# Expert layers of a recurrence-and-two-MoE kernel: second router in common operations for up to four tiles, expert rows in units of 32, sort moved between the two products

## The chip, the cores and the metric

One core of one Trainium2 chip. The metric is the device time of one execution in microseconds (us), the median of several executions.

## The reference, cut to what matters

A recurrence over 768 steps (4 batches, 8 heads of 40) gives 3072 rows of 320 values. Two mixture-of-experts layers follow, each with 8 experts of 320 x 1024 and 1024 x 320 weights, each row going to the expert of its largest logit. The second layer has a capacity of 768 rows per expert.

```python
def _moe_ref(x, w_gate, w_output_gate, w1, w2):
    logits = x @ w_gate
    e_idx = np.argmax(logits, axis=1)
    ...
    for e in range(E):
        mask = e_idx == e
        h = np.maximum(x[mask] @ w1[e], 0.0)
        ye = h @ w2[e]
        out[mask] = gate_w[mask, None] * eom[mask, e, None] * ye

def _moe2_ref(x, w_gate, w1, w2, capacity):
    logits = x @ w_gate
    expert_idx = np.argmax(logits, axis=1)
    probs = softmax(logits)
    gate_w = probs[np.arange(N), expert_idx]
    ...
    # each expert takes its rows in order, up to capacity; out = gate_w * relu(x @ w1[e]) @ w2[e]
```

## The kernel before

The recurrence comes first, in 24 chunks of 128 rows. Each finished chunk is routed for layer 1 (logits, choice of expert, rank within the expert, gate) and scattered by an indirect DMA to its expert's region of a DRAM table, `xs1`. Layer 1 works through this table expert by expert and scatters its rows, routed for layer 2, into `xs2`. Layer 2 does the same and scatters its rows to the output.

**Slots and blocks.** Experts are sorted by their number of rows into 8 slots, and a slot has a fixed number of rows: `NU1` and `NU2` (L721 to L722) count them in units of 64. A slot's rows are cut into blocks of up to four tiles of 128 rows (`Layer`, L764 to L779); the last tile of a block may have 64. The first slot of a layer is cut in two, so that its first block (`HEAD1`, `HEAD2`) can begin before all rows are there. Layer 1 has the blocks 0 to 8 (block 2 is the second slot, block 8 the last), layer 2 the blocks 9 to 18. Rows beyond an expert's count are zero. Were an expert to have more rows than its slot, a branch behind the two layers would compute the rest, tile by tile, with weights loaded anew.

**One block** (`stream`, L1079). The first product (`first`, L1035) has eight steps f = 0 to 7. Each is 8 matmuls (L1050) of a 128 x 128 weight piece with all the block's rows as columns (the high and low parts of an fp32 value are multiplied separately), into one of three PSUM buffers `hp`. ScalarE then writes `hh` (L1052) and VectorE `hl` (L1053). The second product (`second`, L1058) takes the tiles j one by one, with 24 matmuls of 320 columns each (L1072, again eight steps f), into one of two PSUM buffers `yp`. Then the epilogue of the tile runs: ScalarE scales the result into `x2` (L1369), VectorE copies 64 columns to pad it (L1370). In layer 2 ScalarE writes `y` (L1383) and GpSimd scatters it.

**What is put between the steps.** `between(phase, f)` (L1153) runs side work behind the matmuls of step f. The letters are `e` (one step of every waiting router), `l` (load the rows of the next block), `x` (transpose and split a tile of the next block, L1025 to L1029), `w` (convert a third of a weight matrix to high and low parts, L993/L994 and L1006/L1007, then fetch the next third to the freed buffer). `PLAN` (L748) gives the places for blocks 0, 1, 2, 9 and 10. For the others `FT`, `FL`, `FW` give the steps in the first product, and `ST`, `SX`, `SW` those in each tile of the second. `hooks` (L1468) runs the sort of the experts (`order`, L929), the choice of the two leading experts (`leads`, L961) and the table counts (`left`, L1428) before or in the middle of given blocks. From block 0 on every engine, and the queue on which SyncE (SP) issues the DMAs, executes its instructions in the order in which the code issues them.

**The router of layer 2** (`route2` L910, `route` L797) runs for one tile in three steps. First three transposes of `x2` on TensorE (L803) and a copy of the result by ScalarE (L805). Second the logits (three fp32 matmuls, L809, six in the profile) and five VectorE operations to the choice `oh` (L812 to L822). Third two matmuls for the ranks (L832, L833), then ten VectorE operations and an exponential, and the scatter (L919).

## Time and profile before

| | |
|---|---|
| median of 3 executions | 954.26 us (951.37 to 959.03) |
| profiled execution | 947.28 us, of which the span from first to last instruction is 945.5 us |
| mean granted TensorE clock | 0.931 |
| busy: TensorE matmul, weight load | 808.0 us (85%), 716.8 us (76%) |
| busy: VectorE, ScalarE, GpSimd | 665.9 us (70%), 502.5 us (53%), 301.5 us (32%) |
| matmuls of the first product (L1050), second (L1072) | 1216, 1296 |

Times in the profile are us from the start of the span. The recurrence fills some 456 us and overlaps block 0. Block 2 begins at 508.56, block 9 (layer 2) at 727.53, block 10 at 752.61, and the last matmul is at 932. A matmul row shows when it starts and how long it runs, and successive matmuls overlap, so the cost of a matmul in a stream is the distance of the starts.

### The profile page before, as it was taken

The page shows a single profiled execution, that of the slowest core. Times are in us where ns is not written, and L with a number is a line of the kernel's source. Part 1 is how long each engine was busy: PE and PEld are TensorE (multiplying, and loading weights), DVE is VectorE, ACT ScalarE, POOL GpSimd, SP SyncE. Part 2 cuts the span into 40 slices and gives each one's busy share as a digit, 9 for nine tenths or more (in the row PEclk, how much of TensorE's full clock was granted, in tenths as well). Part 3 has the DMA queues.
Part 4 walks back from the last instruction along what each step waited for, and adds up shares of the span by engine and source line. Part 5 has one row for each costly group of instructions (what it writes and reads, how often), then busy time and mean ns, then how long its engine had stood idle before and what let it go on. Part 6 is the DMA issues. An engine that isn't in the chain of part 4 may idle for free. (4 is left out here: it accounts for less than half of the span.)

```text
span 945.5 us, 31326 instructions
## 1 busy us (share of the span) xinstructions
PE 808.0 (85%) x12638; PEld 716.8 (76%) x12638; DVE 665.9 (70%) x1902; ACT 502.5 (53%) x1241; POOL 301.5 (32%) x465
## 2 busy tenths in 40 slices
PE   8357678878879778969999999999899999999994
PEld 4236567756767667757798888999898989999994
DVE  6999966996996976752676767767777844556561
ACT  6225467756857747759443543545355444445551
POOL 8835545645555644223120111111101111101120
PEclk9757789989989879989999999999999999999998
DMA  6759777687665633355353525535445434625640
GB/s 169 195 120 252 212 181 197 174 225 216 162 156 129 154 76 98 89 132 159 115 142 109 151 62 148 141 93 155 132 140 159 140 112 143 193 66 175 180 142 22
DMA packets 132853, 137.50 MB, mean 145 GB/s; under 512 B 68388, under 2 KB 114183, under 8 KB 132700
## 3 DMA queue, kind: packets, MB, share of 16 engines
q1 hardware_dynamic: 128140, 121.99, 48.4%
q0 software_dynamic: 4560, 13.43, 3.9%
q8 instruction: 102, 1.67, 0.8%
q14 instruction: 51, 0.42, 0.1%
HBM read 91.25 MB, written 28.68 MB: 127 GB/s over the span
## 5 line engine op out<-in xcount | busy, mean ns | idle before, releaser
L1072 PE MATMUL yp<-w2h,hh 128*128 128x320 f32 (+1 forms) x432 | 139.4, 327 | 0.6 <-ACT hh L1052 0.6
L919 POOL DMA_INDIRECT xs<-x,di x52 | 55.4, 1065 | 260.2 <-ACT xh L1027 94.9
L1053 DVE SCALAR_TENSOR_TENSOR hl<-hp,hh 128x384 fp32r<-128x384 f32 (+5 forms) x152 | 77.6, 517 | 80.0 <-ACT hh L1052 78.5
L1072 PE MATMUL yp<-w2l,hh 128*128 128x320 f32 (+1 forms) x432 | 132.7, 311 | 0.0
L1050 PE MATMUL hp<-xh,w1h 128*128 128x384 f32 (+5 forms) x456 | 126.3, 335 | 2.7 <-ACT xh L1027 2.1
L1050 PE MATMUL hp<-xh,w1l 128*128 128x384 f32 (+5 forms) x456 | 124.3, 327 | 0.0
L1072 PE MATMUL yp<-w2h,hl 128*128 128x320 f32 (+1 forms) x432 | 112.2, 309 | 0.0
L1052 ACT ACTIVATE hh<-hp 128x384 fp32r<-128x384 f32 (+5 forms) x152 | 68.2, 459 | 81.0 <-PE hp L1050 78.0
L252 DVE TENSOR_TENSOR X<-X,tmp 128x112 f32<-128x112 f32 (+19 forms) x186 | 81.2, 437 | 5.6
L250 DVE TENSOR_TENSOR tmp<-N,X 128x112 f32<-128x112 f32 (+19 forms) x186 | 81.0, 437 | 5.0
L1050 PEld LDWEIGHTS hp<-xh,w1h 128*128 128x128 f32 x456 | 79.8, 191 | 5.5 <-ACT xh L1027 2.6
L1050 PEld LDWEIGHTS hp<-xh,w1l 128*128 128x128 f32 x456 | 81.9, 189 | 2.1
L451 POOL TENSOR_TENSOR YL<-uvs,mlow 64x512 f32<-64x512 f32 x44 | 58.3, 1326 | 76.8 <-ACT uvs L448 70.9
L1072 PEld LDWEIGHTS yp<-w2h,hh 128*128 128x128 f32 (+1 forms) x432 | 79.9, 185 | 2.0 <-ACT hh L1052 0.8
L1072 PEld LDWEIGHTS yp<-w2l,hh 128*128 128x128 f32 (+1 forms) x432 | 79.6, 184 | 0.6
L919 POOL DMA_INDIRECT out_dram<-y,ti x26 | 26.5, 1018 | 165.3 <-DVE ti L1346 32.5
L1050 PE MATMUL hp<-xl,w1h 128*128 128x384 f32 (+5 forms) x304 | 74.8, 327 | 0.4 <-DVE xl L1028 0.2
L1072 PEld LDWEIGHTS yp<-w2h,hl 128*128 128x128 f32 (+1 forms) x432 | 73.8, 183 | 0.4
L102 PE MATMUL ps<-wb 128*128 128x512 bf16 x217 | 72.7, 421 | 1.4 <-POOL wb L95 1.1
L994 DVE TENSOR_TENSOR w1l<-ws,w1h 128x1024 fp32r<-128x1024 f32 x48 | 58.5, 1221 | 20.7 <-ACT w1h L993 14.3
L414 PE MATMUL ps<-consts,T 104*104 104x104 f32 x368 | 46.3, 272 | 19.2 <-ACT KBS L416 17.5
L414 PEld LDWEIGHTS ps<-consts,T 104*104 104x104 f32 x368 | 38.7, 140 | 24.6 <-ACT KBS L416 21.6
(267 smaller groups left out, 1801.3 us busy)
## 6 DMA issues: line engine op xcount, KB each, us to landing
xt<-xs SPq DMA_DIRECT2D x49, 193.0 KB
kb<-in_kb_dram SPq DMA_DIRECT2D x24, 360.0 KB
ws<-in_w_dram SPq DMA_DIRECT2D x16, 512.0 KB
ws<-in_v_dram SPq DMA_DIRECT2D x16, 512.0 KB
xs<-z SPq DMA_DIRECT2D x8, 965.0 KB
KBS<-KBI SPq DMA_DIRECT2D x48, 160.0 KB
ws<-in_w_dram SPq DMA_DIRECT2D x16, 480.0 KB
ws<-in_v_dram SPq DMA_DIRECT2D x16, 480.0 KB
```

The lines of the kernel that those rows point to most:

```text
L102: pin(matmul(wps, wb, wb.unsqueeze(1).to_broadcast([128, 4, 128]), **whole))
L250: nc.vector.tensor_tensor(out=tmp, in0=N[:, j:j + 1, i].to_broadcast([128, m, n]), in1=X[:, k, j:j + 1].to_broadcast([128, m, n]), op=ALU. ...
L252: nc.vector.tensor_tensor(out=X[:, k, i], in0=X[:, k, i], in1=tmp, op=ALU.add)
L414: pin(transpose(sp[0:104, h, 0:104], t1[0:104, i, h0 + h], ident[0:104, 0:104]))
L451: (nc.vector if last else nc.gpsimd).tensor_tensor(out=yl[q, 2 * cl:2 * cl + 2], in0=s[q].rearrange("p (i h t) -> p i h t", i=2, h=H), in1 ...
L919: self.nc.gpsimd.indirect_dma_start(out=dst, out_offset=bass.IndirectOffsetOnAxis(ap=di[:, 0:1], axis=0), in_=src, in_offset=None, bounds_ ...
L994: return lambda: nc.vector.tensor_tensor(out=t["w1l"][:, k], in0=s, in1=t["w1h"][:, k].bitcast(F32), op=ALU.subtract)
L1050: nc.tensor.matmul(hp[:, 0:n], a, b, start=(i == 0), stop=(i == len(ops) - 1))
L1052: nc.scalar.activation(hh[:, f, 0:n], hp[:, 0:n], AF.Relu)
L1053: nc.vector.scalar_tensor_tensor(out=hl[:, f, 0:n], in0=hp[:, 0:n], scalar=0.0, in1=hh[:, f, 0:n].bitcast(F32), op0=ALU.max, op1=ALU.subtract)
L1072: nc.tensor.matmul(yp[0:m, 0:DM], a[:, g, c], w[b][:, g], start=(f == i == 0), stop=(f == 7 and i == 2))
```

## The change

Four things change together.

- Slots are counted in units of 32 rows. Layer 1's slots go from 448, 448, 448, 448, 384, 384, 384, 384 rows to 448, 448, 416, 416, 384, 384, 384, 352. Layer 2's go from 512, 512, 640, 384, 384, 320, 256, 256 to 512, 480, 640, 384, 384, 320, 256, 224. The heads keep 320 and 384 rows. The number of tiles stays 28 and 26, since a short tile is still a tile.
- The second router works on all tiles of a block together. Tile by tile it transposes, now with the logits of the tile before in the same step. When all logits are there, one chain of VectorE operations chooses for up to four tiles, and one pair of rank matmuls, one exponential and one chain of VectorE operations end it. Then come a reciprocal and a scatter for each tile.
- `leads` and `left` run in the middle of their blocks (7 and 3), between the two products, where they ran before them.
- Router steps stand at other places (`FT`, `ST`, `PLAN`), and the load of block 10 moves from step 2 to step 6 of block 9.

```diff
-UNIT = 64
-NU1 = (7, 7, 7, 7, 6, 6, 6, 6)
-NU2 = (8, 8, 10, 6, 6, 5, 4, 4)
-HEAD1, HEAD2 = 5, 6
+UNIT = 32
+PER = 128 // UNIT
+NU1 = (14, 14, 13, 13, 12, 12, 12, 11)
+NU2 = (16, 15, 20, 12, 12, 10, 8, 7)
+HEAD1, HEAD2 = 10, 12
...
-FT, FL, FW = (0, 1, 3), 3, ((), (2, 4, 6))
-ST, SX, SW = (2, 5), (3,), (0, 4)
+FT, FL, FW = (0, 2, 6), 3, ((), (2, 4, 6))
+ST, SX, SW = (2,), (3,), (0, 4)
...
-    9: ({0: 'e', 1: 'e', 2: 'l', 3: 'w', 4: 'w', 6: 'ew', 7: 'w'}, {0: 'w', 1: 'w', 5: 'e', 6: 'x', ...
+    9: ({0: 'e', 2: 'e', 3: 'w', 4: 'w', 6: 'elw', 7: 'w'}, {0: 'w', 1: 'w', 9: 'w', 17: 'w', 20: 'x', 23: 'w'}),
...
+    def route2(self, P, pools, X, tk, n, wg, seen, xs):
+        nc, v = self.nc, self.nc.vector
+        ps, sb = pools
+        lp = ps.tile([128, 512], F32, tag="rt", name="lp")
+        lq, lr = (lp[:, q:q + 8 * n] for q in (384, 416))
+        def logits(j, xT):
+            for k in range(3):
+                self.pin(nc.tensor.matmul(lq[:, 8 * j:8 * j + 8], xT[:, 128 * k:128 * k + 128], wg[:, k], ...
+        turned, xT = 0, None
+        while turned < n:
+            if turned < len(X):
+                if turned:
+                    logits(turned - 1, xT)
+                for k in range(3):
+                    self.pin(nc.tensor.transpose(lp[:, 128 * k:128 * k + 128], X[turned][:, 128 * k:128 * k + 128], self.ident))
+                xT = sb.tile([128, 384], F32, tag="rxT", name="xT")
+                self.pin(nc.scalar.copy(xT, lp[:, 0:384]))
+                turned += 1
+            yield
+        logits(n - 1, xT)
...
+        v.reduce_max(m.unsqueeze(2), lg, axis=AX.X)
+        v.tensor_tensor(out=ex, in0=lg, in1=wide(m), op=ALU.subtract)
+        v.scalar_tensor_tensor(out=sc, in0=ex, scalar=0.0, in1=low, op0=ALU.is_equal, op1=ALU.mult)
+        v.reduce_max(mx.unsqueeze(2), sc, axis=AX.X)
+        v.tensor_scalar(out=va, in0=tk[:, 0:n], scalar1=0.0, scalar2=None, op0=ALU.is_gt)
+        v.tensor_tensor(out=sc, in0=sc, in1=wide(mx), op=ALU.is_equal)
+        v.tensor_tensor(out=oh, in0=sc, in1=wide(va), op=ALU.mult)
+        v.tensor_copy(pre[:, 0], seen)
+        for j in range(n):
+            v.tensor_tensor(out=pre[:, j + 1] if j + 1 < n else seen, in0=pre[:, j], in1=oh[:, j], op=ALU.add)
+        yield
+        self.pin(nc.scalar.activation(ex, ex, AF.Exp))
+        self.pin(nc.tensor.matmul(lr, self.tri, h[:, 0:8 * n], start=True, stop=False))
+        self.pin(nc.tensor.matmul(lr, self.ones, h[:, 32:32 + 8 * n], start=False, stop=True))
+        v.tensor_tensor(out=rk, in0=values(lr), in1=self.ebase.unsqueeze(1).to_broadcast([128, n, NE]), op=ALU.add)
...
+        for j in range(n):
+            v.reciprocal(X[j][:, 384:385], den[:, j:j + 1])
+            self.scatter(xs, di[:, j:j + 1], X[j], NE * REG)
...
-("before", 0, 2, 0): left, ("before", 0, NE - 2, 0): leads,
+("middle", 0, 2, 0): left, ("middle", 0, NE - 2, 0): leads,
```

On SP, block 9 of the program before. `xt<-xs_58` is the load of block 10's rows from layer 2's table, the three `ws` rows below it are the fetches of the next slot's second weight matrix, in thirds of 3, 3 and 2 pieces, and `128x1024` begins a first weight matrix.

```order
L1011 DMA xt<-xs_58 128x386
L1000 ISA
L1000 DMA ws<-in_v_dram 128x3x320
L1000 ISA
L1000 DMA ws<-in_v_dram 128x3x320
L1000 ISA
L1000 DMA ws<-in_v_dram 128x2x320
L783 TENSOR_LOAD l2i
L783 ISA x2
L985 ISA
L985 DMA ws<-in_v_dram 128x1024
```

The same place on SP in the changed program:

```order
L1051 ISA
L1051 DMA ws<-in_v_dram 128x3x320
L1051 ISA
L1051 DMA ws<-in_v_dram 128x3x320
L1062 ISA
L1062 DMA xt<-xs_58 128x386
L1051 ISA
L1051 DMA ws<-in_v_dram 128x2x320
L784 TENSOR_LOAD l2i
L784 ISA x2
L1036 ISA
L1036 DMA ws<-in_v_dram 128x1024
```

The load of block 10's rows moved past two of the three fetches, and the third fetch is now queued behind it.

On VectorE, block 7 of the program before: the end of `leads` (`l2k`, `l2m`), which stands ahead of the block's first `hl`, and a router's third step behind it.

```order
L969 TENSOR_SCALAR l2m<-consts,l2r 128x8
L971 TENSOR_TENSOR l2k<-l2k,l2m 128x8
L1438 COPY fl<-l2k 128x8
L834 TENSOR_TENSOR seen_7913<-seen_7913,oh 128x8
L836 TENSOR_TENSOR rt<-lp,consts 128x8
L837 TENSOR_TENSOR rt<-rt,oh 128x8
L838 TENSOR_REDUCE rt<-rt 128x1
```

The end of `leads` in the changed program, in the middle of the same block. `w1l` is a weight conversion, `xl` and `xh` the split of a tile of the next block, and `x_11629` the padding of the block's first finished tile.

```order
L1020 TENSOR_SCALAR l2m<-consts,l2r 128x8
L1022 TENSOR_TENSOR l2k<-l2k,l2m 128x8
L1495 COPY fl<-l2k 128x8
L1045 TENSOR_TENSOR w1l<-ws,w1h 128x1024
L1079 TENSOR_TENSOR xl<-tp,xh 128x2x128
L1080 TENSOR_TENSOR xh<-tp,xh 64x128
L1045 TENSOR_TENSOR w1l<-ws,w1h 128x1024
L1427 COPY x_11629<-x_11629 128x64
```

Behind `leads` stand now two weight conversions, a split and the padding copy, in place of a router's step. `left` moved likewise in block 3.

## Rows read from the trace of the kernel before

**Rows 1.** Windows: length, busy us (count) of PE, PEld, DVE, ACT, POOL; clock, DMA, GB/s.

```profile
508.56:752.61 244.05, 233.83 (x1510) 218.75 (x1511) 176.85 (x625) 113.25 (x238) 32.99 (x58) 0.99 0.45 130
```

**Rows 2.** Waits of TensorE, 509 to 752.6: waiting <- ended by: us, times, longest.

```profile
PE lp L809 <- DVE va L1377: 4.5, 2, 2.6
PE lp L809 <- ACT xT L805: 1.3, 3, 0.9
PE tp L803 <- DVE x L1370: 1.2, 4, 0.3
PE tp L1025 <- DMA xt<-xs: 0.9, 1, 0.9
PE tp L803 <- DVE rt L836: 0.6, 1, 0.6
PE tp L803 <- DVE l2t L937: 0.6, 1, 0.6
```

**Rows 3.** Timeline of TensorE: start, us, line, op, operands, count.

```profile
660.75 0.31 PE L1072 MATMUL yp<-w2l,hh 128*128 128x320 f32 x1
660.90 0.73 PE L809 MATMUL lp<-consts,xT 128*128 128x8 f32 x6
661.49 0.39 PE L1072 MATMUL yp<-w2h,hh 128*128 128x320 f32 x1
661.72 0.31 PE L1072 MATMUL yp<-w2h,hl 128*128 128x320 f32 x1
...
663.77 0.18 PE L832 MATMUL lp<-oh,tri_b 128*128 128x8 bf16 x1
...
663.84 0.53 PE L803 MATMUL tp<-consts,x 128*128 128x128 f32 x3
664.12 0.39 PE L1072 MATMUL yp<-w2h,hh 128*128 128x320 f32 x1
```

**Rows 4.** Windows, matmuls of L1050 alone: length, busy us (count), granted clock.

```profile
767.35:781.88 14.53, 14.53 (x64) 1.00 0.14 41
796.96:808.05 11.09, 11.09 (x64) 1.00 0.22 73
819.26:826.73 7.47, 7.47 (x64) 1.00 0.66 197
753.40:760.42 7.02, 7.02 (x60) 1.00 0.95 283
```

**Rows 5.** Timeline of VectorE, block 7: first and last of the 14 of leads.

```profile
669.66 0.16 DVE L937 COPY l2t<-lp 128x8 f32<-128x8 f32 x1
...
672.42 0.17 DVE L1438 COPY fl<-l2k 128x8 f32<-128x8 f32 x1
```

**Rows 6.** Groups of VectorE, blocks 2 to 9: count | busy us, mean ns | idle before.

```profile
L994 DVE TENSOR_TENSOR w1l<-ws,w1h 128x1024 fp32r<-128x1024 f32 x24 | 29.4, 1225 | 8.0 <-ACT w1h L993 8.0
L1028 DVE TENSOR_TENSOR xl<-tp,xh 128x256 fp32r<-128x256 f32 (+1 forms) x25 | 10.1, 405 | 2.8 <-ACT xh L1027 2.6
L1029 DVE TENSOR_TENSOR xh<-tp,xh 64x128 fp32r<-64x128 f32 (+1 forms) x25 | 7.2, 287 | 0.5
```

**Rows 7.** Window after TensorE's longest wait, in the columns of rows 1.

```profile
675.30:678.00 2.70, 2.70 (x9) 2.70 (x10) 1.56 (x7) 0.00 (x0) 0.99 (x1) 0.50 0.32 114
```

**Rows 8.** Timelines of GpSimd, SP's queue and ScalarE around block 9.

```profile
709.87 0.97 POOL L919 DMA_INDIRECT xs<-x,di  x1 [4.59 <-DVE hl L1053]
...
712.84 1.54 SPq L1011 DMA_DIRECT2D xt<-xs  x3
...
732.44 0.97 POOL L919 DMA_INDIRECT xs<-x,di  x1 [4.43 <-DVE hl L1053]
...
736.56 0.34 SPq L1011 DMA_DIRECT2D xt<-xs  x1
737.17 6.45 SPq L1000 DMA_DIRECT2D ws<-in_v_dram  x3
...
746.60 0.73 ACT L1006 CAST w2h<-ws 128x640 fp32r<-128x640 f32 x1 [2.09 <-DMA ws<-in_v_dram]
```

More of the change, by code (lines that the diff above doesn't have):

```diff
@@ L775, in __init__ @@
             while u < nu:
-                tiles = -(-(nu - u) // 2)
-                n = min(nu - u, head if r + u == 0 else 2 * -(-tiles // -(-tiles // 4)))
-                self.blocks.append((r, u, [min(2, n - j) * UNIT for j in range(0, n, 2)]))
+                tiles = -(-(nu - u) // PER)
+                n = min(nu - u, head if r + u == 0 else PER * -(-tiles // -(-tiles // 4)))
+                self.blocks.append((r, u, [min(PER, n - j) * UNIT for j in range(0, n, PER)]))
                 u += n
@@ L1073, in second @@
                 between(8 * j + f)
-            late = epilogue(xt, yp[0:m, 0:DM])
+            late = epilogue(xt, yp[0:m, 0:DM], j, len(xts))
             if late:
@@ L1362, in moe_layers, with ep1 @@
     wg2 = ins["wg2_sb"]
-    def ep1(xt, yp):
+    batch = []
+    def ep1(xt, yp, j, n):
         m = xt.shape[0]
-        x2 = P["o"].tile([128, W], F32, tag="x2", name="x2", bufs=5)
-        if m < 128:
-            nc.gpsimd.memset(x2[m:128], 0.0)
+        if j == 0:
+            batch[:] = [], P["o"].tile([128, 4], F32, tag="tk", name="tk", bufs=2)
+        X, tk = batch
+        x2 = P["o"].tile([128, W], F32, tag="x2", name="x2", bufs=6)
+        for q in range(m, 128, 32):
+            nc.gpsimd.memset(x2[q:q + 32], 0.0)
         nc.scalar.activation(x2[0:m, 0:DM], yp, AF.Copy, scale=xt[:, 384:385])
@@ L1371, in ep1, with ep2 @@
         nc.gpsimd.tensor_copy(x2[0:m, 385:386], xt[:, 385:386])
-        def late():
-            va = P["o"].tile([128, 1], F32, tag="va", name="va")
-            if m < 128:
-                nc.gpsimd.memset(va[m:128], 0.0)
-            nc.vector.tensor_scalar(out=va[0:m], in0=xt[:, 385:386], scalar1=0.0, scalar2=None, op0=ALU.is_gt)
-            yield from M.route2(pools, x2, wg2, seen2, xs2, va)
-        return late()
-    def ep2(xt, yp):
+        nc.gpsimd.tensor_copy(tk[0:m, j:j + 1], xt[:, 385:386])
+        for q in range(m, 128, 32):
+            nc.gpsimd.memset(tk[q:q + 32, j:j + 1], 0.0)
+        X.append(x2)
+        return M.route2(P, pools, X, tk, n, wg2, seen2, xs2) if j == 0 else None
+    def ep2(xt, yp, j, n):
         m = xt.shape[0]
@@ L1467, in moe_layers @@
     yield from M.stream(P, (L1, L2), {
-        ("before", 0, 0, 0): beside, ("after", 0, 0, 0): done, ("before", 0, 0, HEAD1): slots1, ("loaded", 0, 0, 0): loaded1, ("before", 0, 2, 0): left, ("before", 0, NE - 2, 0): leads,
+        ("before", 0, 0, 0): beside, ("after", 0, 0, 0): done, ("before", 0, 0, HEAD1): slots1, ("loaded", 0, 0, 0): loaded1, ("middle", 0, 2, 0): left, ("middle", 0, NE - 2, 0): leads,
         ("before", 0, NE - 1, 0): loaded, ("middle", 1, 0, 0): slots})
@@ L1553, in fill @@
             nc.gpsimd.memset(z, 0.0)
-            yield from zero_fill(z, ((xs1, -(-max(NU1) // 2)), (xs2, -(-max(NU2) // 2))), lambda **kw: M.pin(nc.sync.dma_start(**kw)))
+            yield from zero_fill(z, ((xs1, -(-max(NU1) // PER)), (xs2, -(-max(NU2) // PER))), lambda **kw: M.pin(nc.sync.dma_start(**kw)))
         def make_x(c, yp, ct, e):
@@ L1570, in again @@
             nc.vector.memset(work, 0.0)
-            for _ in zero_fill(work[:, 0:W], ((xs1, -(-max(NU1) // 2)), (xs2, -(-max(NU2) // 2))), nc.sync.dma_start):
+            for _ in zero_fill(work[:, 0:W], ((xs1, -(-max(NU1) // PER)), (xs2, -(-max(NU2) // PER))), nc.sync.dma_start):
                 pass
```

23 lines of the change are left out of this document (17 added, 6 removed), and 9 rows, old and new, of the table PLAN.

## The prediction

> **What bounds the kernel now.** I read the busy shares in 40 slices first, then windows block by block, then what TensorE waited for, then the timelines around its waits. The edits lie in blocks 2 to 11 and in block 18. In the 244.05 us from block 2 to block 10 TensorE is busy for 233.83, VectorE for 176.85, ScalarE for 113.25 [rows 1]. The reader is to see a stage limited by TensorE, with 10.2 us in which it idles. So an instruction taken from VectorE counts only where TensorE waited for it, and a column or an insertion taken from TensorE counts in full. Of the idle time 9.1 us end on things that this change touches [rows 2]: 4.5 us on the router's logits behind VectorE's sorts, 1.3 on the copy of the transposed tile, 1.2 on the padding copy, 0.9 on the load of block 9's rows, 0.6 and 0.6 on a PSUM buffer still read by VectorE.
>
> **Fewer columns.** 64 matmuls of the first product take 14.53 us at 512 columns and 11.09 at 384, so 0.227 and 0.173 us each, and 0.42 ns a column [rows 4]. 32 columns less on 64 matmuls are 0.86 us. This applies to blocks 3 and 4 (448 to 416), 8 (384 to 352) and 11 (512 to 480): 3.4 us. Block 18 goes from 256 to 224 columns. A matmul of 256 takes 0.117 us and one of 128 also 0.117 (7.02 / 60) [rows 4], so between them I take nothing. The tiles, and with them the 24 matmuls per tile of the second product, stay 28 and 26, and nothing is saved there.
>
> The rows have a floor of 0.117 us under about 256 columns [rows 4]. The Trainium skill ("TensorE: Matmul & The Clock Gate", Back-to-back issue gap) gives a spacing that falls in proportion to the columns plus some 2.5 ns, and says beside it that with weight loads the spacing is set by both. By the formula alone block 18 would save a further 0.85 us and the sum would be 0.85 lower; the rows do not show that.
>
> **Fewer insertions on TensorE.** Put between matmuls 0.15 us apart, the logits of one tile take 660.90 to 661.49, and the next matmul has 0.23 us in place of 0.15: 0.59 + 0.08 = 0.67 us. The rank pair takes 663.77 to 663.84 (0.07), the transposes to 664.12 (0.28), and the restart costs 0.08 again [rows 3]. Before, a tile costs logits alone (0.67) and ranks with transposes (0.43), 1.10 us, for 28 tiles 30.8. After, a block of n tiles costs transposes alone (0.36), n - 1 times logits with transposes (0.95), logits alone (0.67) and ranks alone (0.15): 1.18 + 0.95 (n - 1). Nine blocks with 28 tiles make 10.6 + 18.1 = 28.7. Saved: 2.1 us.
>
> **Waits that go.** Transposes and logits stand a whole tile apart now, the long VectorE chains leave the second product, and the sorts leave the place in front of the first. I take the 9.1 us away [rows 2] and put what replaces them below. The load of block 9's rows stood in block 8 behind the scatters of block 7's first router steps, and was issued 3.0 us after the last of these (709.87 to 712.84) [rows 8]. Now block 7's scatters come later (step 6) than the load (step 3), and it waits only for older ones. After the longest wait (2.6 us) the granted clock was 0.50 for 2.7 us, that is the 1.2 GHz level [rows 7]. The eight matmuls in it would have taken 8 x 0.173 = 1.4 us, so 1.3 us go with that wait. Sum: 10.4 us.
>
> **Waits that come.** (1) `leads` (14 operations, 669.66 to 672.59, 2.9 us [rows 5]) and `left` (also 14, about as long) now stand at the head of VectorE's work for the second product. Behind them are queued two weight conversions of 1.2 us and a split of 0.4 + 0.3 [rows 6], and then the padding copy that the third transpose of the block's first tile needs: 2.9 + 2.5 + 0.7 = 6.1 us. TensorE arrives there after 24 + 9 matmuls of 0.15 and a transpose group, 5.3 us. VectorE begins late by the ranks of the block before and two `hl`, which I estimate at 1.4 us from operations 0.2 us apart (2.9 / 14). Wait: 6.1 + 1.4 - 5.3 = 2.2 us, bounds 0.8 and 3.0, in two blocks: 4.4.
>
> (2) Block 9. The load of block 10's rows needs all of layer 1's scatters, and these are issued at step 6 now, three in a row. The load stands on SP ahead of the third fetch of the second weight matrix, whose conversion stands on ScalarE ahead of the epilogue of the first tile, and that epilogue frees the `yp` buffer that the third tile needs. Counted from the end of step 6: the rank pair and eight VectorE operations 0.2 apart, 1.6, first scatter there, third 2 us later (0.97 each [rows 8]), 3.6. From a scatter to the load behind it are 3.0 (709.87 to 712.84) to 4.1 (732.44 to 736.56) [rows 8]; the fetch follows 0.6 later (737.17). The third fetch before was issued by 743.62 at the latest and its conversion began at 746.60, so 3.0 us. Conversion 0.73, epilogue 0.5 (estimated for 320 elements from the 0.73 for 640). Sum 11.4 to 12.5. TensorE wants the buffer after the last step of the first product and two tiles, 1.5 + 7.2 = 8.7. Wait 2.7 to 3.8. I take 3.8, the nearer row being block 9's own, and 1.3 for the clock [rows 7]: 5.1. The lower bound is 0, should the scatters land sooner or the first product run late. `slots`, on VectorE in the same place as before, is over by then.
>
> (3) The common chain stands in step 2 of the first product before `hl` of that step, and TensorE needs the buffer `hp` back three steps later. 0.65 (logits) + 12 operations of 0.2 + 0.55 (`hl`, estimated for 384 elements between the 0.405 for 256 and 1.225 for 1024 [rows 6]) = 3.6 us, against 0.67 + 2 steps of 8 x 0.173 = 3.45: up to 0.2 in eight blocks, less where steps are wider. I take 0.6. No trace shows these operations on 24 or 32 elements. Those on 64 elements in `leads` stand no further apart than 0.26, those on 8 no less than 0.2 if they depend on each other, so the bounds are 0 and 6 us.
>
> Reciprocals, scatters and memsets on GpSimd keep their number or lie beside TensorE's work. GpSimd's waits are for others, and only the end of block 9 waits for it.
>
> **Sum.** -3.4 - 2.1 - 10.4 + 4.4 + 5.1 + 0.6 = -5.8 us against the profiled execution of 947.28 (span 945.5 and 1.8 around it): 941.5. That execution lies 7 us under the median of 954.26. On the scale of the median I forecast 948.5, 0.6% less.
>
> **Rivals.** *The new waits are hidden.* Scatters land early, VectorE is ahead of TensorE when the sorts come, and (1) and (2) shrink to 1.8 and 0. For it: VectorE loses more than 200 instructions and is only 72% busy. Against it: each wait is a chain of instructions in a fixed order, and each link has a row. -15.9 + 1.8 + 0.6 = -13.5: 940.8.
>
> *The common chain holds the `hp` buffers.* With x us per wide operation the wait in step 5 is 12x - 2.25, in about eight blocks. At x = 0.25 that is 6 us and eats the gain; at 0.35 it is 2.0 us in eight blocks, 16 in place of my 0.6, so +10 and 964. For it: these operations read PSUM and broadcast operands with three-dimensional patterns, which the rows for 8 elements do not show. Against it: the sorts' operations on 64 elements with broadcasts stand 0.26 apart at most. From 0.25 us per operation on the kernel is slower.
>
> *A slot is too small.* Then the branch behind the layers runs, one tile at a time with all weights anew. Eight first-product steps (7.5 us), a tile (3.5) and the loading of 2.6 MB at the 130 GB/s of rows 1 (20 us) are over 30 us, so 979 or more. Counting the reference's rows for its drawn inputs gives 421, 423, 414, 388, 375, 371, 357, 323 in layer 1's slots (414 of 416 the closest) and 504, 450, 629, 367, 358, 301, 248, 215 in layer 2's, so all fit, provided that the leading experts come out as 504 before 450, as they do with the rows routed by the middle of block 7.
>
> **How the numbers follow.** A measurement of this kernel tells about 1% (9.5 us) from no change. My forecast gets 0.62, the hidden waits 0.26, the held buffers 0.10, the small slot 0.02. The forecast's own range is -11 to +3, from the bounds of (1) and (2) and half of the waits that go. Of it some 0.07 lie beyond -9.5; of the hidden waits nearly all. Faster 0.32, of the held buffers 0.08 and the small slot slower, 0.09, the rest 0.59 within 1%. The range from 938 to 959 is -16 to +5: all of the forecast and the hidden waits, and the lesser part of the held buffers.
>
> **What would show it right or wrong.** In the changed profile: 64 matmuls at 416 columns in 11.9 to 12.0 us and at 224 in 7.2 to 7.5; no wait of TensorE on a logits copy; waits of about 2.2 us on the padding copy in blocks 3 and 7; a wait of SP's queue on the last scatter in block 9, a late third conversion and 3 to 4 us of TensorE's idle time before block 9's third tile; VectorE's common operations 0.2 us apart. Wrong would be: waits in step 5 of every block (the second rival), instructions in the branch at the end (the third), no wait in block 9 (the first), or a time outside 938 to 959.

## The result and the profile after

The changed kernel takes 960.15 us (median of 20 runs, 952.64 to 965.70) where the kernel before took 953.35 on the same chip (median of 20, 944.31 to 961.29). The ratio is 1.0084, 95% interval 1.0059 to 1.0109: 0.8% slower, and 1 us beyond the 959 that closed the predicted range. The profiled execution has 962.65 us, span 960.9. (Here and below a ratio leaves out executions more than 1.5% above the fastest of their kernel, so it can lie off the ratio of the two medians.)

First the page of the changed kernel, its busy times and the row of the granted clock.

```profile
span 960.9 us, 30946 instructions
PE 807.4 (84%) x12600; PEld 724.3 (75%) x12600; DVE 627.0 (65%) x1673; ACT 498.6 (52%) x1194; POOL 313.3 (33%) x507
PEclk9667799979879889989999988999999799999997
```

TensorE is busy for 0.6 us less than before and VectorE for 39 us less, yet the span is 15.4 us longer. So these two engines did not get more to do, and the time went into waiting and into a lower clock behind it (mean 0.911, before 0.931). Of these 15.4 us only some 7 are typical: the profiled execution of the kernel before lies 6 us under its median, and this one 2.5 over. Where the time went, the same window and the same view of waits as [rows 1, 2] show. The window's columns are those of [rows 1]; the stretch from block 2 to block 10 now lies at 507.64 to 767.06.

```profile
507.64:767.06 259.42, 231.21 (x1478) 222.72 (x1477) 144.03 (x427) 110.73 (x196) 44.92 (x97) 0.94 0.46 134
```

```profile
PE lp L929 <- DVE x L1427: 13.3, 2, 11.7
PE yp L1123 <- ACT y L1440: 8.2, 1, 8.2
PE hp L1101 <- DVE hl L1104: 4.0, 1, 4.0
PE lp L929 <- POOL x L1425: 2.5, 1, 2.5
PE hp L1101 <- ACT xh L1078: 0.2, 1, 0.2
```

Before, TensorE idled in this stretch for 10.2 us; now for 28.2, and these rows sum to it. The waits of [rows 2] on the router's logits and on the transposed copy are gone. The names in the new list are VectorE and ScalarE, and one line GpSimd. That is what ended the wait last. What these engines had waited for themselves is the next question, and the waits of VectorE (same view, engine VectorE) answer it for two of the places:

```profile
DVE m1v L1284 <- POOL m1it L1273: 9.7, 1, 9.7
DVE t L947 <- POOL tk L1430: 5.2, 1, 5.2
```

`m1it` is the list 0 to 31 that GpSimd writes for `left` (`tables`, L1273). `tk` is the column of tokens that GpSimd copies in the epilogue (L1430). GpSimd's own timeline at the end of block 2's router shows why both were late (start, us, engine, line, operation, operands, idle time before it and what ended that):

```profile
560.08 0.99 POOL L970 DMA_INDIRECT xs<-x,di  x1 [27.12 <-ACT hh L1103]
563.61 0.97 POOL L970 DMA_INDIRECT xs<-x,di  x1 [2.54 <-ACT w1h L1044]
567.00 0.98 POOL L970 DMA_INDIRECT xs<-x,di  x1 [2.42 <-DMA xs<-x,di]
570.62 0.97 POOL L970 DMA_INDIRECT xs<-x,di  x1 [2.65 <-DMA xs<-x,di]
571.65 0.16 POOL L1273 IOTA m1it<- 128x32 f32 x1
```

The four scatters of a block are ready together now. They write one table, and each waits until the one before has landed: 3.4 to 3.6 us apart, though each occupies GpSimd for under 1.0. GpSimd takes its instructions in order, so the iota stands behind 11 us of scatters. VectorE stands at `left` meanwhile, and behind `left` on VectorE stands the padding copy (L1427, at 576.19) that the transposes of block 3's first tile need. TensorE waits 11.72 us.

The DMA view of the kernel before has the number already (scatters issued from 500 to 760, the count and the median us from issue to landing):

```profile
xs<-x,di POOLq DMA_INDIRECT x27, 3.1
```

The waiting is not new either: the scatter issued there at 573.26 takes 5.3 us to land, the next leaves at 579.34, 0.8 us later, and eight of that kernel's scatters in this stretch stand at that distance behind a landing, as those above do. But there the scatters of single tiles become ready one by one, 5 us and more apart in nearly all blocks, and from block 2 to block 10 TensorE and VectorE wait for GpSimd for 1.3 us in all; in the changed kernel it is 17.4. The Trainium skill ("DMA: Bandwidth & Descriptors", Anatomy of one DMA) gives some 2.0 us per DMA for setup and completion and the rest by bytes, which for the 198 KB of a scatter is an estimate of 2.5 us from that page. The trace agrees within 0.2 us in the quiet stretch above, where the median landing is 2.7 us; the last section shows where it does not.

The other places are the same queue, or SyncE's behind it. In block 2, the copy `tk` stood behind block 0's scatters at 504.75, 511.82 and 518.40. In block 5, the zeros of a 32-row tile (L1425, 625.76) stood behind a scatter at 623.91. In block 9 it went as the prediction says, only longer. Timelines of GpSimd, SP's queue, ScalarE and TensorE; they answer to [rows 8]:

```profile
745.68 1.32 POOL L970 DMA_INDIRECT xs<-x,di  x1 [12.95 <-ACT w2h L1057]
749.45 0.97 POOL L970 DMA_INDIRECT xs<-x,di  x1 [2.45 <-DVE u L997]
752.84 0.97 POOL L970 DMA_INDIRECT xs<-x,di  x1 [2.42 <-DMA xs<-x,di]
...
755.45 0.34 SPq L1062 DMA_DIRECT2D xt<-xs  x1
756.05 0.37 SPq L1051 DMA_DIRECT2D ws<-in_v_dram  x1
...
759.08 0.73 ACT L1057 CAST w2h<-ws 128x640 fp32r<-128x640 f32 x1 [10.04 <-DMA ws<-in_v_dram]
...
760.28 0.64 PE L1123 MATMUL yp<-w2h,hh 128*128 128x320 f32 x1 [8.17 <-ACT y L1440]
```

Third scatter, load of block 10, third fetch, its conversion, the epilogue, and only then TensorE's third tile. After such a wait TensorE runs at half its clock for a while: the granted clock is 0.50 from 576 to 582 and from 760.28 to 766, and 0.98 from 582 to 588. The products in which the two longest waits lie (second of block 3, second of block 9), and for comparison the same two before:

```profile
559.18:591.35 32.17, 20.45 (x130) 19.08 (x130) 13.69 (x37) 10.45 (x17) 6.86 (x19) 0.79 0.37 114
744.64:767.06 22.42, 14.25 (x77) 13.75 (x77) 11.98 (x51) 4.33 (x7) 4.24 (x4) 0.77 0.57 175
```

```profile
560.19:579.66 19.47, 19.13 (x140) 17.80 (x139) 15.34 (x53) 10.73 (x21) 1.61 (x3) 1.00 0.55 158
740.83:752.61 11.78, 11.23 (x77) 10.96 (x77) 10.10 (x41) 5.74 (x11) 1.80 (x1) 1.00 0.37 109
```

Block 3's second product has grown by 12.7 us, block 9's by 10.6, block 2's first by 5.2, block 5's first by 4.1: 32.6 us lost at four places. Elsewhere, up to block 18's last product, the kernel won 21 us on balance. From the start of that product to the end of the span it takes 2.2 us more than before, and block 0 began 1.8 us later; together with the 32.6 lost and the 21 won these make the 15.4.

### The profile page after: what moved, and what is told of

The parts are those of the page before. It is cut to its first block, busy times and chain, and to the rows that moved or that the text cites. A ratio compares the mean times of both kernels' runs of the same rounds, so it can differ in the third digit from the quotient of the medians.

```text
span 960.9 us, 30946 instructions
## 1 busy us (share of the span) xinstructions
PE 807.4 (84%) x12600; PEld 724.3 (75%) x12600; DVE 627.0 (65%) x1673; ACT 498.6 (52%) x1194; POOL 313.3 (33%) x507
## 4 chain that ended last, share of the span: by engine, by line
PE 56%; DVE 24%; DMA 7%; issue 6%; ACT 4%; SPq 1%; POOL 1%; POOLq 0%; DVEq 0%; ACTq 0%
PE hp L1101 19%; PE yp L1123 16%; DVE tmp L250 4%; DVE X L252 4%; DMA xs<-x,di 3%; PE ps L102 2%; PE ps L395 2%; PE ps L435 2%; PE tp L1076 2%; DVE cex L172 2%; PE ps L444 2%; DVE rex L181 2%; PE ps L367 2%; PE ps L414 1%; PE ps L237 1%
## 5 line engine op out<-in xcount | busy, mean ns | idle before, releaser
L1123 PE MATMUL yp<-w2h,hh 128*128 128x320 f32 (+3 forms) x432 | 139.5, 327 | 8.2 <-ACT y L1440 8.2
L1104 DVE SCALAR_TENSOR_TENSOR hl<-hp,hh 128x384 fp32r<-128x384 f32 (+8 forms) x152 | 75.4, 506 | 93.4 <-ACT hh L1103 88.4
L1123 PE MATMUL yp<-w2l,hh 128*128 128x320 f32 (+3 forms) x432 | 133.6, 313 | 0.0
L1101 PE MATMUL hp<-xh,w1h 128*128 128x384 f32 (+8 forms) x456 | 125.7, 333 | 6.2 <-DVE hl L1104 4.4
L1101 PE MATMUL hp<-xh,w1l 128*128 128x384 f32 (+8 forms) x456 | 123.1, 324 | 0.0
L1123 PE MATMUL yp<-w2h,hl 128*128 128x320 f32 (+3 forms) x432 | 114.3, 314 | 0.0
L1123 PEld LDWEIGHTS yp<-w2h,hh 128*128 128x128 f32 (+3 forms) x432 | 80.2, 186 | 9.2 <-ACT y L1440 8.4
L1101 PEld LDWEIGHTS hp<-xh,w1h 128*128 128x128 f32 x456 | 79.7, 191 | 9.2 <-DVE hl L1104 5.1
L1101 PEld LDWEIGHTS hp<-xh,w1l 128*128 128x128 f32 x456 | 82.1, 190 | 1.2
L1123 PEld LDWEIGHTS yp<-w2l,hh 128*128 128x128 f32 (+3 forms) x432 | 79.9, 185 | 0.9
L1123 PEld LDWEIGHTS yp<-w2h,hl 128*128 128x128 f32 (+3 forms) x432 | 74.5, 185 | 1.0 <-DVE hl L1104 0.2
L1101 PE MATMUL hp<-xl,w1h 128*128 128x384 f32 (+8 forms) x304 | 74.3, 326 | 0.5 <-DVE xl L1079 0.5
```

Of the source, the lines that this page charges most:

```text
L1101: nc.tensor.matmul(hp[:, 0:n], a, b, start=(i == 0), stop=(i == len(ops) - 1))
L1104: nc.vector.scalar_tensor_tensor(out=hl[:, f, 0:n], in0=hp[:, 0:n], scalar=0.0, in1=hh[:, f, 0:n].bitcast(F32), op0=ALU.max, op1=ALU.subtract)
L1123: nc.tensor.matmul(yp[0:m, 0:DM], a[:, g, c], w[b][:, g], start=(f == i == 0), stop=(f == 7 and i == 2))
```

## The experiments

All are cut from the changed kernel, except 8 and 10. Theory: a block's scatters wait for each other's landing, and the queues of GpSimd and SyncE hand that on. Rivals: the place of `left` and `leads` in the middle of a block, the width of the common operations, the short tiles. Experiments 5 and 10 leave some output rows unwritten. Each experiment has 4 to 12 executions, of which one is profiled. The ratio is to the kernel before, with its 95% interval, and the table gives for the profiled execution the length in us of the products that matter, from the start of a product's first matmul to the next product's (timeline of TensorE).

| | ratio | block 1, both | 2 first | 3 second | 5 first | 9 second | 10 first |
|---|---|---|---|---|---|---|---|
| before | 1 | 17.9 | 14.7 | 19.5 | 13.0 | 11.8 | 7.9 |
| changed | 1.0084 | 15.0 | 19.9 | 32.2 | 17.0 | 22.4 | 7.4 |
| 1 iota early | 0.9957 (0.9929 to 0.9986) | 15.0 | 21.7 | 19.8 | 16.4 | 21.4 | 7.4 |
| 2 fetch ahead | 1.0101 (1.0060 to 1.0143) | 15.0 | 21.7 | 31.6 | 14.8 | 18.9 | 7.4 |
| 3 on VectorE | 1.0047 (1.0013 to 1.0080) | 19.5 | 14.0 | 30.9 | 13.1 | 22.3 | 7.4 |
| 4 all three | 0.9912 (0.9871 to 0.9953) | 19.6 | 14.0 | 19.8 | 13.1 | 19.0 | 14.1 |
| 5 scatters apart | 0.9869 (0.9803 to 0.9935) | 15.0 | 14.2 | 25.1 | 13.1 | 13.5 | 7.4 |
| 6 router earlier | 0.9982 (0.9955 to 1.0009) | 19.8 | 14.0 | 19.8 | 13.1 | 18.5 | 14.2 |
| 7 `left` in front | 0.9943 (0.9906 to 0.9980) | 15.0 | 22.1 | 17.6 | 15.6 | 21.3 | 7.4 |
| 8 units alone | 1.0008 (0.9975 to 1.0041) | 19.2 | 14.7 | 19.4 | 12.9 | 11.8 | 7.9 |
| 9 block 8 by tiles | 0.9889 (0.9849 to 0.9930) | 19.0 | 14.0 | 19.9 | 13.1 | 19.9 | 14.1 |
| 10 units, hooks | 0.9992 (0.9964 to 1.0020) | 19.0 | 14.7 | 21.6 | 12.9 | 11.8 | 7.9 |
| 11 load moved too | 0.9834 (0.9796 to 0.9871) | 15.0 | 14.2 | 21.4 | 13.1 | 11.0 | 7.4 |

**1. The iota early.**

```diff
-        nc.gpsimd.iota(T["it"], ...
+        if name != "m1": nc.gpsimd.iota(T["it"], ...
...
     def done():
         ...
-        M.mp = sbuf("mp")
+        M.mp = sbuf("mp"); M.it1 = M.mp.tile([128, 32], F32, name="m1it"); nc.gpsimd.iota(M.it1, ...)
```

> The iota of `left` (L1273) is issued by GpSimd when block 0 ends, ahead of every scatter of layer 1; nothing else differs from the changed kernel. Theory (GpSimd's order: the iota stood behind block 2's four scatters, VectorE waited 9.7 us for it, TensorE 11.7): VectorE's wait for the iota goes, the second product of block 3 is 10 to 12.7 us shorter, the other three places keep their loss, and the ratio to the kernel before falls from 1.008 to 0.996 to 0.998. Rival (the fourteen operations of `left` in the middle of the block are themselves what TensorE waits for, as `leads` in block 7): TensorE still waits for the padding copy (L1427) in block 3 for 8 us or more, and the ratio stays at 1.004 to 1.010.

As the theory has it: 19.8 for block 3's second product, ratio 0.996. One instruction of 0.16 us, put a few lines earlier, takes back 12 us. What is left of TensorE's waits on the padding copy:

```profile
PE lp L929 <- DVE x L1427: 3.6, 2, 2.0
```

2.0 in block 3 and 1.6 in block 7: this is the price of the two sorts in the middle, forecast at 2.2 each. The rival is out.

**2. The third fetch ahead of the load.**

```diff
-    9: ({0: 'e', 2: 'e', 3: 'w', 4: 'w', 6: 'elw', 7: 'w'}, ...
+    9: ({0: 'e', 2: 'e', 3: 'w', 4: 'w', 6: 'ewl', 7: 'w'}, ...
```

> In block 9 the conversion with its fetch goes ahead of the load of block 10 on SyncE; nothing else differs from the changed kernel. Theory (the load waits for block 8's scatters, each of which waits for the landing of the one before, and holds the third fetch behind it on SyncE's queue): the fetch leaves before 741, TensorE's wait of 8.2 us at the first output of block 9 goes and the clock of that stretch rises above 0.90; the second product of block 9 is 8 to 11 us shorter and the ratio 0.997 to 1.000. Rival (the block's epilogue or the load itself is late whatever the fetch does): the wait moves to the transposes of block 10 and the ratio stays at 1.005 to 1.010.

A miss: the rival holds. The wait on the epilogue is gone, and another of 6.2 us takes its place, behind the same product's third tile:

```profile
756.44 0.88 PE L1076 MATMUL tp<-consts,xt 128*128 128x128 f32 x3 [6.20 <-DMA xt<-xs]
```

Block 10's rows cannot be loaded before block 8's last scatter has landed (issued at 750.51, load at 753.59), whatever stands around the load. The gain is 3.5 us in the product and none that the ratio shows.

**3. The small operations on VectorE.** In `ep1`, the four `nc.gpsimd.` (L1425, L1428, L1430, L1432) become `nc.vector.`.

> The four small operations of the epilogue (L1425, L1428, L1430, L1432: zeros of a short tile, two copies of a column, zeros of the column) go from GpSimd to VectorE; nothing else differs from the changed kernel. Theory (they stand behind scatters in GpSimd's queue; `va` waited 5.2 us for one of them in block 2, the transposes 2.5 us in block 5): the waits of TensorE at 521 and 625 go, block 2's first product is 4 to 5 us shorter and block 5's 3 to 4, VectorE gets some 5 us of work in all over ten blocks; block 3 and block 9 keep their loss; ratio 0.999 to 1.003. Rival (the common chain on VectorE is itself too long, and more work on VectorE makes it longer): both waits stay or grow, ratio 1.007 to 1.013.

Blocks 2 and 5 behave as expected, 14.0 and 13.1. Block 1 does not: 19.5 in place of 15.0, with the clock at 0.76 in its first product, which no theory had. TensorE's waits there are 0.28 and 0.24 us. I put it down to the zeros of block 0's short tile, which now stood on VectorE ahead of the padding copy, and gave them back to GpSimd in experiments 9 and 11. Experiment 9 has the low clock all the same and 11 has not, with the same instructions up to block 9, so the zeros are not shown to be the cause. The whole time, 1.0047, is above the 0.999 to 1.003 expected.

**4. All three together.**

> The three edits together (iota early, fetch ahead of the load, small operations on VectorE), the rest as in the changed kernel. Theory (GpSimd's queue behind the scatters is the common cause of the four waits): the losses add up, so the ratio is 1.008 less 0.012, 0.010 and 0.008: 0.976 to 0.984, which is 930 to 938 us where the kernel before has 953, and what is left is what the columns and the removed waits were forecast to give. Rival (the widths of the common operations or the shorter tiles cost what the change cost): 0.995 or more.

Faster than the kernel before, 0.991, but short of the 0.984 expected. In the profiled execution the table says where: 4.6 us of low clock in block 1, and in block 9 the wait of experiment 2, behind which the clock stayed low for the whole of block 10's first product (14.1 in place of 7.4). That execution, 947.39 us, is the longest of six; the shortest took 936.16, and whether the shorter ones have the low clock too no trace shows. The losses of blocks 2, 3 and 5 are all removed; that of block 9 has changed its form.

**5. Scatters that don't wait for each other.**

```diff
-            self.scatter(xs, di[:, j:j + 1], X[j], NE * REG)
+            self.scatter([xs, *self.apart][j], di[:, j:j + 1], X[j], NE * REG)
...
+        M.apart = [tc.dram_tile([NE * REG, W], F32, name="xa%d" % j) for j in range(3)]
```

> The changed kernel, but a block's second, third and fourth scatter write three other tables, so that no scatter of a block waits for the landing of the one before; the rows of these tiles are left out of layer 2, whose instructions stay the same. Theory (the waits of 3.4 us and more between a block's scatters hold GpSimd's queue, and this is what the four places of TensorE's idle time share): scatters of a block stand 1.0 to 1.3 us apart; VectorE's wait for the iota falls from 9.7 to 1 to 3 us and block 3's second product from 32.2 to 20 to 24; the load of block 10 lands 7 us earlier and block 9's second product falls from 22.4 to 12 to 16; block 2's first product from 19.9 to 15 to 17 and block 5's from 17.0 to 13 to 15. Ratio 0.980 to 0.990. Rival (the scatters are slow by themselves, descriptors made by GpSimd one after the other, whatever they wait for): spacing stays above 3 us, ratio 1.004 to 1.010.

GpSimd's timeline at the place shown above for the changed kernel:

```profile
551.20 0.99 POOL L970 DMA_INDIRECT xs<-x,di  x1 [27.11 <-DVE hl L1104]
552.49 0.98 POOL L970 DMA_INDIRECT xa<-x,di  x1 [0.30 <-DVE fl L1474]
553.77 0.97 POOL L970 DMA_INDIRECT xa<-x,di  x1 [0.30 <-issue]
555.05 0.97 POOL L970 DMA_INDIRECT xa<-x,di  x1 [0.31 <-issue]
556.08 0.16 POOL L1273 IOTA m1it<- 128x32 f32 x1
```

1.28 us apart, the iota 4.9 us behind the first scatter instead of 11.6, VectorE's wait for it 2.8 us in place of 9.7. All four places shrink at once, with the iota and the small operations where the change had put them. That the waits for landings are the common cause is shown for blocks 2, 3 and 5. In block 9 the gain has a second source: the load of block 10's rows waits here for one scatter of block 8 and not for three. Block 3 keeps somewhat more than expected (25.1, expected 20 to 24): TensorE still waits 5.0 us for the padding copy, and the clock is 0.50 in the 5 us behind it.

**6. Block 8's router earlier, the load and the transposes later.**

```diff
-    9: ({0: 'e', 2: 'e', 3: 'w', 4: 'w', 6: 'ewl', 7: 'w'}, {0: 'w', 1: 'w', 9: 'w', 17: 'w', 20: 'x', 23: 'w'}),
+    9: ({0: 'e', 1: 'e', 3: 'w', 4: 'ew', 6: 'w', 7: 'w'}, {0: 'w', 1: 'wl', 9: 'w', 17: 'w', 23: 'wx'}),
```

> The three edits of the fourth run, and block 9 written anew: block 8's router gets its steps behind f = 0, 1 and 4 instead of 0, 2 and 6, the load of block 10 is issued in the second product, and block 10's rows are transposed in step 23 instead of 20. What was left in the fourth run is TensorE's wait of 6.2 us for block 10's rows, the half clock behind it (14.06 us in place of 7.37 for block 10's first product). Theory (it waits for block 8's scatters, one landing after the other): the scatters go 3.5 us earlier and the transposes 1.6 us later, the wait falls to 1 us or less, the clock stays full, block 9's second product takes 13 to 15 us and block 10's first 7.4: the ratio falls from 0.991 by 0.010 to 0.013, to 0.978 to 0.982. Rival (block 10's rows would wait whatever the order, or an earlier second half of the router makes TensorE wait for VectorE in block 9's first product): a wait of 3 us or more in block 9, ratio 0.987 or more.

(The edit is against experiment 4.) The rival again: still 6.2 us of waiting for block 10's rows. Against the start of block 9's second product, the first scatter came 3.6 us earlier than in experiment 4 and the third only 1.5:

```profile
723.83 1.33 POOL L970 DMA_INDIRECT xs<-x,di  x1 [10.91 <-ACT hh L1103]
731.10 0.98 POOL L970 DMA_INDIRECT xs<-x,di  x1 [5.94 <-DVE fl L1475]
734.53 1.73 POOL L970 DMA_INDIRECT xs<-x,di  x1 [2.45 <-DVE ni L1522]
```

The second stands 7.3 us behind the first, with the DMA engines 75% busy in between; the third 3.4 behind the second, at 24%. A fixed 3.4 per scatter, as I had reckoned here, is too little beside weight fetches. The third took 6.0 us to land, and SyncE's queue stood at the load until it had (load at 740.62):

```profile
SPq L1062 <- DMA xs<-x,di: 3.1, 1, 3.1
```

**7. `left` in front of block 3 again.** The hook's place goes from `"middle"` back to `"before"`.

> The changed kernel with `left` hooked before block 3 again, as in the kernel before; `leads` stays in the middle of block 7. Theory (the iota then stands ahead of block 2's scatters; `left` on VectorE ahead of the first product costs the transposes' split, some 2 us): block 3's second product falls from 32.2 to 20, its first grows by 2 to 3 us, ratio 0.998 to 1.001, a little above the run with the early iota alone (0.996). Rival (the place in the middle of the block was itself the loss): ratio below that of the early iota, 0.994 or less.

0.994, below the 0.998 to 1.001 expected, and block 3's first product did not grow at all (13.9, expected 2 to 3 more). With the common router the sort costs nothing in front of the first product, and 2.2 us in the middle (17.6 against experiment 1's 19.8). So in the profiles `left` in the middle loses even without the iota; the whole time of experiment 1, 0.996, lies within this one's interval and does not tell the two apart.

**8. Units of 32 alone.** The constants of the change in the kernel before, with (16, 16, 20, ...) for layer 2, and zeros written 32 rows at a time.

> The kernel before with rows in units of 32 alone (second slot of layer 2 at 16 units), its own router, plan and hooks. Theory (as in the prediction, the columns are worth 3.4 us on TensorE, and short tiles cost GpSimd two memsets more): the first products of the shortened blocks are shorter by 0.02 us for each 4 columns and matmul as forecast, nothing else moves, ratio 0.994 to 0.998. Rival (shorter tiles lose as much as they gain, in weight loads and in more memsets ahead of the transposes): ratio 0.999 to 1.003.

The blocks agree with the theory: blocks 3, 4 and 8 have first products shorter by 0.48, 0.80 and 0.64 us, block 7 by 1.5, blocks 17 and 18 by 1.0 together, block 1 is 1.3 longer in both products, and blocks 0 to 18 up to the last product are together 3.2 us shorter. The whole time does not show it: 1.0008, the rival's number, and the interval begins at 0.9975. Part of the answer stands behind the last matmul: from there to the end of the span are 12.9 us before and 14.7 here. All twelve profiles with units of 32 have this, 1.7 to 2.3 us more from the start of block 18's second product to the end, against the one profile of the kernel before. The 1.5 us that remain are 0.2%, and lie within the interval.

**9. Block 8 routed tile by tile.** Experiment 4, with GpSimd keeping the small operations in block 0, and

```diff
+        if M.at == 8:
+            j, n = 0, 1
...
-    9: ({0: 'e', 2: 'e', 3: 'w', 4: 'w', 6: 'elw', 7: 'w'}, {0: 'w', 1: 'w', ...
+    9: ({0: 'e', 2: 'e', 3: 'w', 4: 'ew', 6: 'w', 7: 'w'}, {0: 'w', 1: 'wl', ...
```

> The changed kernel with three things: the iota early (as in the first run), the four small operations of the epilogue on VectorE except in block 0, where GpSimd has no scatters (there the zeros of the short tile came 0.7 us later on VectorE and its clock fell, 4.6 us), and block 8 alone with the second router tile by tile (steps behind every second and fifth f, the last tile's behind f = 0, 2 and 4 of block 9), the load of block 10 issued in the second product. Theory (the batch is harmful where somebody waits for all scatters soon, which is block 10's load; elsewhere it only needs a free GpSimd queue): block 8's scatters stand 3 us and more apart without waiting, the last at 722 to 726, TensorE's wait for block 10's rows goes; block 9's second product takes 12 to 13.5 us and block 10's first 7.4, blocks 1 and 2 lose no clock. From the fourth run's table: 18.98 + 14.06 less 20 is 13 us, blocks 1 and 2 give 4.6: the ratio is 0.991 less 0.018, 0.970 to 0.978. Rival (the load of block 10 is late for another reason, such as the weights' traffic): TensorE waits 3 us or more in block 9, 0.985 or more.

The scatters came in time, the last at 724.86, 2.4 us ahead of block 9's second product (in experiment 4 it came 9.7 us into it). The wait for block 10's rows was 7.3 us all the same, and SP's queue tells why:

```profile
728.86 8.73 SPq L1036 DMA_DIRECT2D ws<-in_v_dram  x3
737.80 0.47 SPq L1038 DMA_DIRECT2D ws<-in_v_dram  x1
738.53 5.61 SPq L1062 DMA_DIRECT2D xt<-xs  x8
```

The last scatter had landed by 730.5 (5.6 us after its issue). But I had put the load behind fetches of the next weights, the last of which left at 737.80. Between the first of them and the second the queue stood for 6.1 us at the reading of `ni`, counts that `slots` writes on VectorE:

```profile
SPq L1534 <- DVE ni L1524: 6.1, 1, 6.1
```

Experiment 6 had the load at the same place, but there the fetches were out by 737.3 and the last landing, at 740.5, came later. The 0.989 lies within the interval of experiment 4. It is no firm gain: the twelve executions run from 935.35 to 954.96, and the medians of all, 946.33 and 949.22 before, have a ratio of 0.997. The profiled execution, 949.37, is the seventh of the twelve.

**10. Units and hooks, without the common router.** Experiment 8 with `left` and `leads` in the middle. Some output rows stay unwritten in it, and which is not known; against experiment 8 only the two hooks stand elsewhere, and the number of instructions is the same, so its blocks can be compared with those of 8.

> The kernel before with rows in units of 32 (as in the eighth run) and both hooks, `left` and `leads`, in the middle of their blocks; its router stays tile by tile. Theory (the hooks in the middle cost little as long as no batch of scatters stands ahead of the iota): block 3's first product falls by 2 to 2.5 us and block 7's by 3, against 1 to 2.5 us more in each of their second products; ratio 0.996 to 1.000. No wait of VectorE for the iota above 2 us. Rival (the sort in the middle is itself the loss): block 3's second product grows by 5 us or more, ratio 1.004 or more.

The theory: block 3's first product loses 2.3 us and its second gains 2.2, block 7's first loses 2.8 and its second gains 2.0. VectorE never waits for the iota. The sorts in the middle are harmless where scatters come singly, and the 0.9992 is within what was expected.

**11. The load ahead of the fetches.**

```diff
-    9: ({0: 'e', 2: 'e', 3: 'w', 4: 'ew', 6: 'w', 7: 'w'}, {0: 'w', 1: 'wl', ...
+    9: ({0: 'e', 2: 'e', 3: 'w', 4: 'ew', 6: 'wl', 7: 'w'}, {0: 'w', 1: 'w', ...
```

> The ninth run with one DMA moved: the load of block 10 is issued in the first product of block 9 behind the conversion of step 6, ahead of the next weight fetches on SyncE, instead of behind them. The ninth run's profile has block 8's last scatter at 724.9, 11 us ahead of the fourth run's on the scale of block 9, and still a wait of 7.3 us for block 10's rows: the load stood on SyncE behind three fetches that waited for a buffer until 736.9. Theory (queue order on SyncE is what is left): the load leaves at 728 to 730, the wait for block 10's rows goes, the clock stays full; block 9's second product 12 to 13.5 us instead of 19.9, block 10's first 7.4 instead of 14.1: ratio 0.989 less 0.013, 0.972 to 0.980. Rival (the fetches that now stand behind the load are late instead): a wait of 3 us or more for weights in blocks 9 to 11, ratio 0.985 or more.

No wait for rows or weights is left in block 9's second product: 11.0, and block 10's first 7.4. The load now leaves at 732.61, ahead of the fetches:

```profile
725.09 5.35 SPq L1051 DMA_DIRECT2D ws<-in_v_dram  x3
732.61 0.35 SPq L1062 DMA_DIRECT2D xt<-xs  x1
733.81 6.53 SPq L1036 DMA_DIRECT2D ws<-in_v_dram  x3
```

935.78 us (median of 6) against 950.14, ratio 0.9834: the lowest ratio of all, though the interval (0.9796 to 0.9871) overlaps those of 5 and 9, and faster than both kernels, though not the 0.972 to 0.980 expected. Of what the table shows against experiment 9, the 4 us of block 1 are no gain of the edit, as the instructions are alike there. The stretch from block 2 to block 10, in the columns of [rows 1]:

```profile
510.68:741.02 230.34, 224.37 (x1482) 216.51 (x1481) 154.48 (x523) 111.83 (x198) 32.20 (x28) 0.99 0.49 144
```

230.3 us, against 244.1 before and 259.4 with the change as it was.

## Why the prediction was wrong

**Fewer columns: right.** The first products' own matmuls (windows of L1101 alone) in blocks 3, 4, 8 and 11 of the changed kernel:

```profile
545.28:559.18 13.90, 12.77 (x64) 11.58 (x64) 1.00 0.10 34
591.35:605.19 13.84, 12.71 (x64) 11.61 (x64) 1.00 0.11 35
705.80:717.98 12.18, 11.05 (x64) 10.13 (x64) 1.00 0.56 153
781.03:794.90 13.87, 13.87 (x64) 11.83 (x64) 1.00 0.16 47
```

The first three were 13.64, 13.62 and 11.92 before, so 0.87, 0.91 and 0.87 less, forecast 0.86; block 11 has 0.66 less. Sum 3.3, forecast 3.4. Block 18 gained 0.2 at most (7.64 for 224 columns; its own 256 columns took 7.87 before, block 13's 7.47 in [rows 4]), close to the nothing read from the floor in [rows 4]. The formula of the Trainium skill ("TensorE: Matmul & The Clock Gate", Back-to-back issue gap), which that page gives for a matmul by itself, would have been an estimate of 0.85 less; the trace does not show it. My mark of 11.9 to 12.0 for 416 columns was for matmuls with nothing between them; with the router's insertions it is 12.7.

**Insertions and waits that go: right or better.** Outside the four places blocks 0 to 18, up to the last product, became 21 us shorter, with the 1.6 us that `leads` cost already counted against it. The terms said 3.4 + 2.1 + 10.4 = 15.9. The terms were not measured apart, and 2.9 of the 21 us are block 1's, which the prediction did not count.

**Waits that come.** (1) `leads` cost 1.6 us in block 7, and `left` 2.0 as soon as its iota was early (experiment 1): 3.6, forecast 4.4. But for `left` I counted its 14 operations on VectorE and not the iota on GpSimd, for which the first VectorE operation of `count_tiles` waits. (2) In block 9 the chain was the right one and its size wrong: TensorE waited 8.2 us where I had 3.8. The step that failed reads "first scatter there, third 2 us later". It takes the 0.97 us that a scatter occupies GpSimd for the distance to the next. The distance goes by the landing, 3.4 to 3.8 us here and 7.2 from the first to the third, although the 3.0 to 4.1 from a scatter to the load behind it stood in the same paragraph: a second scatter to the same table waits no less than a load from it. (3) The common chain cost nothing of note, and its operations stand 0.2 us apart (`va` on VectorE aside, which waited for `tk`). The second rival is out, as is the third.

**The step that decided it** is the sentence "GpSimd's waits are for others, and only the end of block 9 waits for it". The change makes scatters come in threes and fours, and behind them in GpSimd's queue stand the iota, the token columns and the zeros of short tiles, all of which somebody upstream of TensorE needs soon. Experiments 1 and 3 remove the queueing and 5 removes the waits themselves; 1 and 3 give back what the theory gives them at blocks 2, 3 and 5, and 5 gives back all but 5.7 us of block 3. That is 22 of the 32.6 us lost, a term that the prediction put at nothing. Block 9's 10.6 begin at the same waits for landings, and there SyncE's queue adds its own: the load waits for them, and the third fetch stands behind the load. The tail behind the last matmul, 2.2 us, had no term either. The rival on the slow side that I wrote down had another mechanism, which did not occur.

**What stays open.** Why the span ends 2 us later behind the last matmul with units of 32; why the low clock lasted so differently (below); and a common router whose scatters are spread without giving up the batch was not tried.

## What to carry to other kernels

In this kernel several scatters that write one table cost their landing each (3.4 us apart in quiet stretches, up to 7 beside fetches), not their issue (0.97). Multiply the landing by their number, and list what stands behind them on the engine that issues them and who waits for that. When operations are put together into a batch, look for what the batch now does at one moment that it did spread out before: GpSimd's queue waited for landings before too, but hardly anything that was needed stood behind them. A wait that is removed uncovers the next in the same chain (experiments 2, 6 and 9), so follow the chain to its end before pricing the removal.

## What the hardware showed unexpectedly

A scatter's landing follows the traffic around it. With the DMA engines 15% busy (560 to 571) a block's scatters stood 3.4 to 3.6 us apart. Between 504.75 and 518.40, with the share at 0.66, they stood 7.1 and 6.6 apart.

The clock was not the same for the same work. Experiments 2 and 4 both wait 6.2 us for block 10's rows. Block 9's second product and block 10's first, of experiment 2 and then of experiment 4:

```profile
740.56:759.48 18.92, 12.72 (x78) 12.29 (x78) 11.90 (x51) 4.40 (x7) 5.68 (x5) 0.82 0.46 137
759.48:766.85 7.37, 7.37 (x69) 7.37 (x68) 2.04 (x7) 2.47 (x8) 0.97 (x1) 1.00 1.00 272
```

```profile
726.41:745.39 18.98, 12.76 (x78) 12.32 (x77) 11.91 (x51) 4.52 (x7) 6.02 (x5) 0.89 0.45 141
745.39:759.45 14.06, 14.06 (x69) 14.06 (x68) 2.04 (x7) 2.47 (x8) 0.98 (x1) 0.50 0.54 158
```

In one, block 10's first product runs at full clock; in the other it runs at 0.50, the 1.2 GHz level, to its end, 6.7 us more. Block 1's first product shows the same without a long wait, in experiment 9 and then in 11, whose instructions are alike up to there:

```profile
490.28:502.54 12.26, 11.87 (x88) 11.69 (x85) 8.37 (x42) 3.55 (x12) 0.00 (x0) 0.79 0.10 27
```

```profile
495.69:506.25 10.56, 9.58 (x87) 9.33 (x85) 7.57 (x35) 3.55 (x12) 0.00 (x0) 1.00 0.12 32
```

I have no row that explains either difference. Experiments 9 and 11 have the same instructions up to block 9, so what differs there comes from the execution and not from the edit, and the twelve executions of experiment 9 alone range from 935.35 us at a mean clock of 0.923 to 954.96 at 0.900. Experiment 2's profile is the shortest of its four executions, experiment 4's the longest of its six. So one profile's clock in a single block is no proof of what an edit did there; that blocks 2, 3, 5 and 9 lose their waits is read from the waits and from the whole times.
